# Moving clearing transfers and DRAM copies, and splitting the routing's and norm's small operations, in an mLSTM and mixture-of-experts kernel

## The chip, the cores and the metric

The kernel runs on one NeuronCore of a Trainium2 chip. The metric is device time in microseconds (us) for one execution; smaller is better. The core has a matrix engine (PE, TensorE), a vector engine (DVE), a scalar engine (ACT), a general engine (POOL, GpSimd) and a sequencer that mostly issues transfers (SP); each takes its own instructions in program order, and they wait for each other through semaphores. In the profile PE's clock stands at one of two levels, 2.4 GHz (granted clock 1.00) or 1.2 GHz (0.50).

## What is computed

Three layers follow each other. The reference, cut to its core (B=2, H=8, S=768, D=40, so 1536 tokens of 320 numbers; 8 experts):

```python
for t in range(S):                                    # an mLSTM, per batch and head
    m_new = maximum(f[t] + m, i[t]); f_s = exp(f[t] + m - m_new); i_s = exp(i[t] - m_new)
    C = f_s * C + i_s * outer(v[t], k[t]);  n = f_s * n + i_s * k[t]
    y[t] = sigmoid(o[t]) * (C @ q[t]) / maximum(abs(n @ q[t]), 1.0)
logits = x @ w_gate + log1p(exp(x @ w_noise)) * noise # router: two experts per token
out[token] = sum over its top 2 of weight * (relu(x @ w1[e]) @ w2[e])
final = (silu(x @ w_gate2) * (x @ w_val)) @ w_out     # a dense gated layer, 1536 wide
```

## The kernel before

**Attention.** The two sequences are cut into 12 chunks of 128 tokens (6 each, `j` from 0 to 11). A chunk is computed in the parallel form of the mLSTM, and a state is carried from chunk to chunk. The order of the work is written out by hand: strings of letters (`START`, `SECOND`, `BODY`, `LAST`, lines 61 to 65), in which a letter issues one piece for this chunk or for one that lies ahead. For chunk `j`, PE computes the scores `pS` (L275, one chunk ahead), the part from the carried state `py` (L297), the part within the chunk `pY` (L312) and the state's update (L322). ACT computes the weights `W` by an exponential from the broadcast gates `gbt` (`prep_w`, L265, two chunks ahead). DVE multiplies scores by weights (`weigh`, L281), adds the parts to `y` (`norm`, L338 to L344, where a maximum and a reciprocal make the divisor `dn`) and writes the chunk's output `x` in two multiplications (L355 and then L350). PE then transposes `x` (`gate_t`, L363) and multiplies it by the router's weights (`gate_l`, L372); the result is copied to `lg` (L373). In PE's order the transpose of chunk `j-1` stands ahead of `pY` of chunk `j`, so `pY` waits for `x` of the chunk before.

**Gates.** Running sums of the gates, `G_`, are written to DRAM as `gp` (four transfers, L206) and read back, broadcast to all partitions, as `gbt` (L176, from chunk 2 on).

**Routing.** After every three chunks `route` (L376) makes a list of 14 pieces: scale, noise, maxima, indices, one-hot, counts, PE's `place` (a prefix sum by small matmuls, L423 to L430), slots, weights. The letter `d` (`drip`, L486) issues the next piece. A piece holds up to six DVE instructions, and many read what the one ahead of them wrote. The last list is issued among the first steps of the experts, as the numbers in `SEQ` (L53) say. When a token's slot is known, POOL scatters its row to the expert's rows `xs` in DRAM (`scatter`, L474; letter `c`), two rows per token.

**Transfers.** SP issues nearly all transfers, in order, and waits ahead of many for a semaphore. Beside the loads of q and k (`QK`, L166), keys and values (`kvt`, L170), `gbt` and the expert weights (`stg`, L524), these are the clearing of `xs` with zeros (`clear`, L946: eight transfers of 384 rows and one of 320, letter `z`) and a copy of every chunk's output to DRAM (`keep`, L494, into `xd`). `xd` is read only where more tokens choose an expert than it has rows.

**Experts and dense layer.** 80 steps (10 groups of rows, 8 steps each, `step`, L901) and then 36 steps of the dense layer. The first step follows `xprep(0)` (L609), which transposes the rows `xgt` that were loaded back from `xs` (`xload`, L602) when the first 12 scatters had landed. POOL computes the low halves of some weight pieces (`wU`, `wV`, L542) already in the attention.

Of the kernel before, what the change touches and what calls it, by code (L numbers as in the profile page):

```python
# [23 lines left out]
E = 8  # L24
# [10 lines left out]
KD = 1  # L35
# [7 lines left out]
XL = 10  # L43
DU = (0, 1, 2)
# [16 lines left out]
START = 'gffhqkQlffffffff1cfrffff2dffsffffxoOffSffff34WKfTy5Gmfnafwfe6ffffŇŷ7ũŗŋűzųŮŭŶť'  # L61
LV = ()
SECOND = 'dGzcWSdiwydddqcdKactpcdsdnmvcldecd'
BODY = 'GKzcWSdiwddctpqdyacdsdnmdvclcdde'
LAST = 'iyddatdnpdmcdeslccdd'
# [23 lines left out]
def kernel(ctx, tc, qk, kvh, og, gates, cst, wgn, noise, w1, w2, w13, w2o, out):  # L89
# [286 lines left out]
    def route(t0, t1):  # L376
# [3 lines left out]
        def tile(shape, name, dt=F32):  # L380
            return rt.tile(shape, dt, name=f"{name}{n}", bufs=2)
# [14 lines left out]
        def noisy():
            v.tensor_tensor(out=Lg, in0=ex, in1=nz[:, t, :], op=OP.mult)
            v.tensor_tensor(out=Lg, in0=Lg, in1=lg[:, t, 0:E], op=OP.add)

        def top():  # L400
            for i in range(n):
                v.max(mx[:, i, :], Lg[:, i, :])

        def top_index():
            for i in range(n):
                v.max_index(ix[:, i, :], mx[:, i, :], Lg[:, i, :])

        def onehot():
            v.tensor_copy(xf, ix[:, :, 0:2])
            v.tensor_tensor(out=d, in0=mx[:, :, 1], in1=mx[:, :, 0], op=OP.subtract)  # L410
            v.tensor_tensor(out=oh[:, t].rearrange("p j k e -> p (j k) e"),
                            in0=iota_e[:, None, :].to_broadcast([128, 2 * n, E]),
                            in1=xf.rearrange("p j k -> p (j k)")[:, :, None].to_broadcast([128, 2 * n, E]),
                            op=OP.is_equal)

        def chosen():
            v.tensor_tensor(out=sel[:, t], in0=oh[:, t, 0], in1=oh[:, t, 1], op=OP.add)
            v.tensor_copy(selb[:, t], sel[:, t])
# [23 lines left out]
        def limits():  # L442
            v.tensor_tensor(out=pol[:, t], in0=ps_[0], in1=lim_c[:, b, None, :].to_broadcast([128, n, E]), op=OP.is_ge)
            v.tensor_tensor(out=pb, in0=ps_[0], in1=base_c[:, b, None, :].to_broadcast([128, n, E]), op=OP.add)

        def pick(k, src):
            def run():
                v.tensor_tensor(out=tm, in0=oh[:, t], in1=src().to_broadcast([128, n, 2, E]), op=OP.mult)
                v.tensor_reduce(so[:, k], tm, axis=AX.X, op=OP.add)
            return run  # L450
# [33 lines left out]
    spot = [0, 0]  # L484
# [416 lines left out]
    def step():  # L901
# [105 lines left out]
    def early_piece(j):  # L1007
# [10 lines left out]
        "n": (0, norm), "e": (0, emit_a), "m": (0, emit_b),  # L1018
# [12 lines left out]
    for j in range(NJ):  # L1031
# [8 lines left out]
        if j >= KD:  # L1040
            keep(j - KD)
# [128 lines left out]
```

## Time and profile before

| | |
|---|---|
| median of 3 runs | 558.68 us (554.36 to 561.88) |
| the profiled execution | 555.08 us, with a span of 553.4 us from its first to its last instruction |
| busy share of the span | PE 96%, DVE 68%, ACT 50%, POOL 26% |
| mean granted clock of PE | 0.959 |
| instructions | 9232 |
| bytes moved | 96.63 MB, mean 175 GB/s |

The profile is of one execution. A row of a timeline has the start in us from the beginning of the span, the busy time in us, engine, line, operation, what is written and from what, and a count of merged instructions; in brackets stands how long the engine had been idle and what ended that. The rows for a stretch give the busy time of each engine, PE's granted clock (1.00 is 2.4 GHz), the busy share of the DMA engines and the GB/s moved. A busy PE need not be a fast one: at a clock of 0.50 the same matmul is busy about twice as long.

### The profile page before, as it was taken

Reading aid. Unit: us, or ns where it says so; the run is one execution under the profiler, and the core shown is the slowest. Engines: PE = TensorE matmul, PEld = TensorE weight load, DVE = VectorE, ACT = ScalarE, POOL = GpSimd, SP = SyncE. Lnnn points to the kernel's source line nnn. Section 1 sums busy time; section 2 is a strip of 40 time slices with the busy share of each in tenths; the row PEclk is TensorE's granted clock in tenths of the full one; section 3 lists DMA queues with packets and bytes.
Section 4 is the critical chain, followed back from the end, with each engine's and each line's share of the span. In section 5 each row is a group of like instructions: output and inputs, shape, how many; then the busy total and the mean of one; then the engine's idle time right before and its main releaser. Section 6 shows DMA issues by size and latency. Waiting matters only on the chain. (4 is left out here: it accounts for less than half of the span.)

```text
span 553.4 us, 9232 instructions
## 1 busy us (share of the span) xinstructions
PE 529.3 (96%) x3333; PEld 478.8 (87%) x3335; DVE 373.8 (68%) x833; ACT 275.5 (50%) x593; POOL 145.2 (26%) x175
## 2 busy tenths in 40 slices
PE   8998779889999999999999999999999999999997
PEld 4687678879898999989999999888888888888886
DVE  5584977858688897989898867787643434443332
ACT  5464545235566776876877664554332223222221
POOL 4153675455004432232322235233000000000000
PEclk8798877969999999999999999999999999999999
DMA  8799965553758787988987686461001000010001
GB/s 247 214 332 356 304 236 161 168 196 113 295 171 320 259 281 255 330 296 277 317 292 254 214 280 227 160 233 49 0 1 49 0 1 0 2 47 1 1 0 47
DMA packets 36882, 96.63 MB, mean 175 GB/s; under 512 B 4848, under 2 KB 17936, under 8 KB 36832
## 3 DMA queue, kind: packets, MB, share of 16 engines
q1 hardware_dynamic: 32208, 83.55, 44.9%
q0 software_dynamic: 2304, 7.87, 4.3%
q10 hardware_dynamic: 2320, 4.58, 2.4%
q8 instruction: 27, 0.44, 0.3%
q14 instruction: 23, 0.19, 0.1%
HBM read 72.70 MB, written 23.28 MB: 173 GB/s over the span
## 5 line engine op out<-in xcount | busy, mean ns | idle before, releaser
L678 PE MATMUL py<-wV,h 128*128 128x320 f32 (+1 forms) x624 | 106.6, 312 | 1.2 <-ACT ysb L689 0.8
L678 PEld LDWEIGHTS py<-wV,h 128*128 128x128 f32 (+1 forms) x624 | 95.6, 185 | 2.7 <-ACT ysb L689 1.2
L641 PE MATMUL ph<-xh,wU 128*128 128x416 f32 (+1 forms) x320 | 91.5, 336 | 0.4 <-PEq L719 0.4
L581 POOL TENSOR_TENSOR cq<-cq,csg 128x512 f32<-128x512 f32 (+1 forms) x27 | 38.5, 1425 | 121.0 <-ACT cq L580 96.7
L839 DVE TENSOR_TENSOR sg<-pg,sg 128x512 f32<-128x512 f32 x36 | 24.9, 691 | 58.2 <-ACT sg L838 58.2
L860 PE MATMUL py<-wV,uh 128*128 128x320 f32 x288 | 63.8, 309 | 0.0
L641 PEld LDWEIGHTS ph<-xh,wU 128*128 128x128 f32 x320 | 59.6, 195 | 2.5 <-ACTq L719 0.7
L542 DVE TENSOR_TENSOR wU<-stg,wU 128x512 fp32r<-128x512 f32 x72 | 54.1, 776 | 6.7 <-ACT wU L541 6.2
L838 ACT ACTIVATE sg<-pg 128x512 f32<-128x512 f32 x36 | 21.5, 598 | 66.0 <-PE pg L641 61.2
L848 ACT ACTIVATE uh<-u 128x512 fp32r<-128x512 f32 x36 | 22.8, 633 | 62.0 <-DVE u L840 62.0
L641 PE MATMUL ph<-xl,wU 128*128 128x416 f32 (+1 forms) x160 | 52.3, 327 | 0.1
L860 PEld LDWEIGHTS py<-wV,uh 128*128 128x128 f32 x288 | 49.5, 188 | 3.0
L641 PE MATMUL pg<-x2h,wU 128*128 128x512 f32 x144 | 51.4, 397 | 0.0
L641 PE MATMUL pv<-x2h,wU 128*128 128x512 f32 x144 | 50.6, 392 | 0.0
L541 ACT ACTIVATE wU<-stg 128x512 fp32r<-128x512 f32 x78 | 46.4, 624 | 7.4 <-DVE yt L687 4.6
L650 ACT ACTIVATE h<-ph 128x416 fp32r<-128x416 f32 (+1 forms) x80 | 35.6, 445 | 19.5 <-PE ph L641 17.6
L860 PE MATMUL py<-wV,ul 128*128 128x320 f32 x144 | 44.4, 309 | 0.0
L542 DVE TENSOR_TENSOR wV<-stg,wV 128x640 fp32r<-128x640 f32 x42 | 37.6, 906 | 3.4 <-ACT wV L541 3.3
L641 PE MATMUL ph<-xr,wU 128*128 128x416 f32 (+1 forms) x160 | 39.3, 327 | 0.3 <-DVE wU L542 0.3
L849 DVE TENSOR_TENSOR ul<-u,uh 128x512 fp32r<-128x512 f32 x36 | 24.9, 690 | 19.9 <-ACT uh L848 19.9
L777 POOL DMA_INDIRECT gy<-yg,ig__89 x24 | 25.2, 1051 | 48.0 <-DVE wU L542 26.8
L840 DVE TENSOR_TENSOR u<-pv,sg 128x512 f32<-128x512 f32 x36 | 24.9, 691 | 17.1 <-PE pv L641 16.7
(175 smaller groups left out, 1065.6 us busy)
## 6 DMA issues: line engine op xcount, KB each, us to landing
stg<-in_w_dram SPq DMA_DIRECT2D x20, 768.0 KB
stg<-in_w_dram SPq DMA_DIRECT2D x20, 640.0 KB
cw<-in_w_dram SPq DMA_DIRECT2D x18, 512.0 KB
gbt<-gp SPq DMA_DIRECT2D x10, 512.0 KB
f<-cq SPq DMA_DIRECT2D x18, 256.0 KB
stg<-f SPq DMA_DIRECT2D x6, 768.0 KB
kvt<-in_kvh_dram SPq DMA_DIRECT2D x12, 324.0 KB
QK<-in_qk_dram SPq DMA_DIRECT2D x24, 160.0 KB
```

Of the source, the lines that this page charges most:

```text
L541: s.activation(hi[:, c], ST[u][:, c], AF.Copy)
L542: (g if lo_pool[0] else v).tensor_tensor(out=lo[:, c], in0=ST[u][:, c], in1=hi[:, c], op=OP.subtract)
L581: g.tensor_tensor(out=q, in0=q, in1=sg, op=OP.mult)
L641: pe.matmul(ps_ap, a, b, start=(i == 0), stop=(i == len(seq) - 1))
L650: s.activation(h[:, 0:C], p[:, 0:C], AF.Relu)
L678: pe.matmul(yp[0:nr, 0:DM], x_, w, start=st and i == 0, stop=sp and i == 2)
L777: g.indirect_dma_start(out=y, out_offset=None, in_=yg[0:NR0] if j < NC else yg, in_offset=bass.IndirectOffsetOnAxis(ap=ig_[:, j, k:k + 1], ...
L839: v.tensor_tensor(out=sg, in0=pg, in1=sg, op=OP.mult)
L840: v.tensor_tensor(out=u, in0=pv, in1=sg, op=OP.mult)
L848: s.activation(uh, u, AF.Copy)
L849: v.tensor_tensor(out=ul, in0=u, in1=uh, op=OP.subtract)
L860: pe.matmul(OP_[q][a][:, 0:DM], x_[:, t], w[:, c], start=(f == 0 and i == 0), stop=(f == 11 and i == 2))
```

## The change

It has three parts. **(1)** Four of the nine clearing transfers are issued right behind the first loads (`zz` in `START`); the two that stood at the end of `START` go, and later chunks issue 2, 2 and 1 in place of 2, 3 and 2. **(2)** The twelve copies to `xd` during the attention become two of 768 rows each, issued at steps 13 and 17 of the experts. **(3)** `route` returns about 36 single instructions, some of them empty places that only keep distance, in place of 14 pieces, and their order is new; the divisor's maximum and reciprocal (`norm_max`, `norm_rec`) are letters of their own; the strings have more `d`. `SEQ` is not changed.

```diff
-KD = 1
+KX = (13, 17)
-START = 'gffhqkQlffffffff1cfrffff2dffsffffxoOffSffff34WKfTy5Gmfnafwfe6ffffŇŷ7ũŗŋűzųŮŭŶť'
+START = 'gffhqkQlzzffffffff1cfrffff2dffsffffxoOffSffff34WKfTy5Gmfnafwfe6ffffŇŷ7ũŗŋűųŮŎōŭŶť'
-BODY = 'GKzcWSdiwddctpqdyacdsdnmdvclcdde'
+BODY = 'GKzcWSdiwdctpqdydacdsdndNmdMdvclcdedd'
...
-        v.reciprocal(dn, dn)
-        YN[j] = (y, dn)
+    def norm_rec(j):
+        dn = YN[j][1]
+        v.reciprocal(dn, dn)
...
-        return [scale, noisy, top, top_index, onehot, chosen, place, limits, pick(0, lambda: pol[:, t, None, :]),
-                pick(1, lambda: pb[:, :, None, :]), slots, carry, gap_exp, weights]
+        return [scale, None, tt(Lg, ex, nz[:, t, :], OP.mult), tt(Lg, Lg, lg[:, t, 0:E], OP.add), *tops,
...
+                lambda: s.activation(e2, d, AF.Exp),
+                tt(sel[:, t], oh_[:, :, 0], oh_[:, :, 1], OP.add),
+                lambda: v.tensor_copy(selb[:, t], sel[:, t]), total, place,
+                lambda: v.tensor_scalar(d, e2, 1.0, 1e-9, op0=OP.add, op1=OP.add),
+                *([tt(cs, cry, cs, OP.add)] if t0 else []),
+                lambda: v.reciprocal(wk_[:, :, 0], d), None,
...
+                tt(wk_[:, :, 1], e2, wk_[:, :, 0], OP.mult), slots, carry,
...
     def drip(k, last=False):
-        spot[0] += 1
         for _ in range(k):
-            if drq and (last or drq[0].__name__ != "place" or spot[0] > spot[1] + 1):
-                if drq[0].__name__ == "chosen":
-                    spot[1] = spot[0]
-                drq.pop(0)()
+            while last and drq and drq[0] is None:
+                drq.pop(0)
+            if drq:
+                f = drq.pop(0)
+                if f:
+                    f()
-    def keep(j):
-        sy.dma_start(xd[j * 128:(j + 1) * 128, :], x[:, j, 0:DM])
+    def keep(b):
+        sy.dma_start(xd[b * S:(b + 1) * S].rearrange("(j p) d -> p j d", p=128), x[:, b * NC:(b + 1) * NC, 0:DM])
...
+        if i in KX:
+            keep(KX.index(i))
...
-        if j >= KD:
-            keep(j - KD)
```

SP's order at the start of the program, before; the names are the transfers' targets and sources, `gp` and `gbt` the gates, `xs` the rows that are cleared:

```order
L170 DMA kvt<-in_kvh_dram 128x648
L206 DMA gp<-G__120 16x128 x3
L206 DMA gp<-G__120 16x3x128
L176 DMA gbt<-gp 128x1024
L166 DMA QK_113<-in_qk_dram 40x1024 x2
L170 DMA kvt<-in_kvh_dram 128x648
L985 DMA wg_t<-in_wgn_dram 128x3x16
L986 DMA nz<-in_noise_dram 128x96
L176 DMA gbt<-gp 128x1024
L166 DMA QK_111<-in_qk_dram 40x1024 x2
L949 DMA xs<-zt 384x1x320 x2
L170 DMA kvt<-in_kvh_dram 128x648
```

and the same place after the change:

```order
L171 DMA kvt<-in_kvh_dram 128x648
L942 DMA xs<-zt 384x1x320 x4
L207 DMA gp<-G__120 16x128 x3
L207 DMA gp<-G__120 16x3x128
L177 DMA gbt<-gp 128x1024
L167 DMA QK_113<-in_qk_dram 40x1024 x2
L171 DMA kvt<-in_kvh_dram 128x648
L978 DMA wg_t<-in_wgn_dram 128x3x16
L979 DMA nz<-in_noise_dram 128x96
L177 DMA gbt<-gp 128x1024
L167 DMA QK_111<-in_qk_dram 40x1024 x2
L171 DMA kvt<-in_kvh_dram 128x648
```

Four clearing transfers now stand ahead of the gates' way through DRAM, and none stands ahead of the fourth `kvt`.

DVE's order between the score product of chunk 6 (`W`, x2) and `y` of chunk 5, before (`so`, `nov`, `is_`, `cs`, `d`, `wk` are the routing's small tiles of the first three chunks):

```order
L281 TENSOR_TENSOR W_658<-pS,W_658 128x512 x2
L448 TENSOR_TENSOR tm_652<-oh,pb_650 128x48
L449 TENSOR_REDUCE so_651<-tm_652 128x6
L453 TENSOR_SCALAR nov_649<-so_651 128x6
L454 TENSOR_TENSOR so_651<-so_651,nov_649 128x6
L455 TENSOR_TENSOR so_651<-so_651,ck 128x6
L456 TENSOR_TENSOR is__88<-so_651 128x6
L434 TENSOR_REDUCE cs_653<-sel 128x8
L440 CAST cry<-cs_653 128x8
L304 TENSOR_TENSOR t_810<-py,eg 128x328
L463 CAST ig__89<-so_651 128x6
L464 TENSOR_SCALAR d_654<-e_655 128x3
```

(three more routing instructions follow ahead of `y`), and the same place after the change, from `W` on to `x`:

```order
L282 TENSOR_TENSOR W_656<-pS,W_656 128x512 x2
L420 TENSOR_TENSOR sel<-oh 128x24
L305 TENSOR_TENSOR t_789<-py,eg 128x328
L448 CAST selb<-sel 128x24
L426 TENSOR_REDUCE cs_650<-sel 128x8
L339 TENSOR_TENSOR y<-pY,t_789 128x328
L343 TENSOR_SCALAR dn<-y 128x8
L449 TENSOR_SCALAR d_651<-e_652 128x3
L348 TENSOR_TENSOR dn<-dn,y 128x8
L362 TENSOR_TENSOR x<-x,y 128x320
L451 RECIPROCAL wk<-d_651 128x3
L352 RECIPROCAL dn<-dn 128x8
```

Of the routing, 13 instructions stood between `W` and `y`; three do now, and the slots (`is_`) have moved to the chunk after this one.

DVE's order around the fourth step of the experts (the second `h` row below is that step's), before:

```order
L655 SCALAR_TENSOR_TENSOR h<-ph,h 128x224 x2
L397 TENSOR_TENSOR Lg_1439<-ex_1438,nz 128x24
L398 TENSOR_TENSOR Lg_1439<-Lg_1439,lg 128x24
L402 MAX mx_1440<-Lg_1439 128x8 x3
L406 MAX_INDEX ix_1441<-mx_1440,Lg_1439 128x8 x3
L409 CAST xf_1442<-ix_1441 128x6
L410 TENSOR_TENSOR d_1448<-mx_1440 128x3
L411 TENSOR_TENSOR oh<-ck,xf_1442 128x48
L417 TENSOR_TENSOR sel<-oh 128x24
L418 CAST selb<-sel 128x24
L655 SCALAR_TENSOR_TENSOR h<-ph,h 128x224
```

and after the change:

```order
L646 SCALAR_TENSOR_TENSOR h<-ph,h 128x224 x2
L420 TENSOR_TENSOR Lg_1424<-ex_1423,nz 128x24
L420 TENSOR_TENSOR Lg_1424<-Lg_1424,lg 128x24
L438 MAX mx_1425<-Lg_1424 128x8 x3
L439 MAX_INDEX ix_1426<-mx_1425,Lg_1424 128x8
L646 SCALAR_TENSOR_TENSOR h<-ph,h 128x224
L439 MAX_INDEX ix_1426<-mx_1425,Lg_1424 128x8 x2
L442 CAST xf_1427<-ix_1426 128x6
L420 TENSOR_TENSOR d_1433<-mx_1425 128x3
L420 TENSOR_TENSOR oh<-ck,xf_1427 128x48
L420 TENSOR_TENSOR sel<-oh 128x24
L448 CAST selb<-sel 128x24
```

The step's `h` now stands ahead of seven routing instructions that end in `selb`, the input of PE's `place`; PE's own order is the same here, `place` behind the fourth step.

## Rows read from the trace of the kernel before

**Rows 1.** Stretches: busy us per engine (count), PE's clock, DMA share, GB/s

```profile
core 0: us, PE busy (x) PEld busy (x) DVE busy (x) ACT busy (x) POOL busy (x), PEclk, DMA share, GB/s
12.00:16.00 4.00, 3.67 (x17) 3.50 (x19) 3.83 (x8) 4.00 (x3) 1.39 (x1) 0.50 0.50 153
...
28.00:58.00 30.00, 26.16 (x258) 23.97 (x254) 19.41 (x63) 16.85 (x53) 13.95 (x18) 0.89 0.98 335
...
58.00:116.00 58.00, 47.12 (x428) 43.09 (x425) 47.72 (x171) 26.14 (x78) 34.30 (x48) 0.85 0.60 199
...
131.00:553.00 422.00, 415.42 (x2423) 381.59 (x2421) 282.81 (x512) 214.05 (x418) 82.10 (x77) 1.00 0.46 156
```

**Rows 2.** Timeline of PE, the transpose of chunk 5's output

```profile
69.99 0.87 PE L363 MATMUL pg<-ck,x 128*128 128x128 f32 x3 [4.48 <-DVE x L350]
```

**Rows 3.** Stretches in which PE's clock stood at the lower level, columns as in rows 1

```profile
67.41:74.24 6.83, 4.25 (x23) 4.20 (x25) 3.46 (x12) 1.11 (x2) 6.21 (x11) 0.50 0.70 265
81.06:91.30 10.24, 10.24 (x68) 9.38 (x68) 8.65 (x42) 4.16 (x13) 3.96 (x5) 0.50 0.49 150
115.20:125.44 10.24, 9.78 (x40) 9.09 (x41) 4.10 (x22) 1.90 (x6) 5.94 (x12) 0.50 0.75 253
```

**Rows 4.** Timeline of SP's queue, two answers for short windows

```profile
17.06 0.38 SPq L176 DMA_DIRECT2D gbt<-gp  x1
...
28.15 0.36 SPq L170 DMA_DIRECT2D kvt<-in_kvh_dram  x1
```

**Rows 5.** Timeline of ACT, the weights of chunks 2 and 5

```profile
26.62 2.43 ACT L265 ACTIVATE W<-gbt,bc 128x128 f32<-128x128 f32 x8
...
44.68 2.45 ACT L265 ACTIVATE W<-gbt,bc 128x128 f32<-128x128 f32 x8 [4.30 <-DMA gbt<-gp]
```

**Rows 6.** DMA issues by line, count and size of one

```profile
xs<-zt SPq DMA_DIRECT2D x8, 480.0 KB
...
xd<-x SPq DMA_DIRECT2D x12, 160.0 KB
```

**Rows 7.** Timeline of DVE, small instructions that do and do not follow one another

```profile
56.25 0.30 DVE L402 MAX8 mx<-Lg 128x8 f32<-128x8 f32 x3
...
68.35 0.17 DVE L342 TENSOR_SCALAR dn<-y 128x8 f32<-128x8 f32 x1
68.56 0.17 DVE L343 TENSOR_TENSOR dn<-dn,y 128x8 f32<-128x8 f32 x1
```

**Rows 8.** Timeline of DVE from chunk 4's output to chunk 6's

```profile
60.82 0.48 DVE L350 TENSOR_TENSOR x<-x,dn 128x320 f32<-128x320 f32 x1
...
64.88 2.43 DVE L464 TENSOR_SCALAR d<-e 128x3 f32<-128x3 f32 x1
...
69.36 0.49 DVE L350 TENSOR_TENSOR x<-x,dn 128x320 f32<-128x320 f32 x1
...
75.61 1.42 DVE L342 TENSOR_SCALAR dn<-y 128x8 f32<-128x8 f32 x1
...
78.91 0.80 DVE L350 TENSOR_TENSOR x<-x,dn 128x320 f32<-128x320 f32 x1
```

**Rows 9.** Timeline of POOL beside the long instruction of rows 8

```profile
65.72 1.54 POOL L542 TENSOR_TENSOR wV<-stg,wV 128x640 fp32r<-128x640 f32 x1
```

**Rows 10.** Timelines of DVE, POOL, SP and PE: from chunk 9 to the experts

```profile
99.64 0.49 DVE L338 TENSOR_TENSOR y<-pY,t 128x328 f32<-128x328 f32 x1
...
100.11 0.99 POOL L476 DMA_INDIRECT xs<-x,is__88  x1 [0.17 <-issue]
...
102.64 1.74 SPq L607 DMA_DIRECT2D xgt<-xs  x4
...
113.21 0.81 PE L624 MATMUL pxt<-ck,xgt 128*128 128x128 f32 x6
115.57 0.87 PE L363 MATMUL pg<-ck,x 128*128 128x128 f32 x3 [1.56 <-DVE x L350]
```

**Rows 11.** Timelines of DVE and PE at the fourth step of the experts

```profile
126.83 0.39 DVE L655 SCALAR_TENSOR_TENSOR h<-ph,h 128x224 fp32r<-128x224 f32 x1 [0.18 <-ACT h L650]
...
127.11 0.19 PE L423 MATMUL pr<-selb,slt 128*128 128x24 bf16 x1
```

More of the change, by code (lines that the diff above doesn't have):

```diff
@@ L390, in route @@
         ps_ = []
+        oh_, wk_ = oh[:, t], wk[:, t]
+        ohr = oh_.rearrange("p j k e -> p (j k) e")
         def scale():
@@ L394, in scale @@
             s.activation(ex, ex, AF.Ln, bias=1.0)
[L396 to L418, printed above, removed]
         def place():
@@ L431, in place, with tt, limit, total @@
                           start=False, stop=True, skip_group_check=True)
+        def tt(out, in0, in1, op):
+            return lambda: v.tensor_tensor(out=out, in0=in0, in1=in1, op=op)
+        def limit(out, lim, op):
+            return lambda: v.tensor_tensor(out=out, in0=ps_[0], in1=lim[:, b, None, :].to_broadcast([128, n, E]), op=op)
+        def total():
+            v.tensor_reduce(cs, sel[:, t].rearrange("p j e -> p e j"), axis=AX.X, op=OP.add)
         def carry():
-            v.tensor_reduce(cs, sel[:, t].rearrange("p j e -> p e j"), axis=AX.X, op=OP.add)
-            if t0:
-                v.tensor_tensor(out=cs, in0=cry, in1=cs, op=OP.add)
             if t1 == NC:
@@ L440, in carry @@
                 v.tensor_copy(cry, cs)
[L442 to L450, printed above, removed]
@@ L469, in route @@
-        return [scale, noisy, top, top_index, onehot, chosen, place, limits, pick(0, lambda: pol[:, t, None, :]),
-                pick(1, lambda: pb[:, :, None, :]), slots, carry, gap_exp, weights]
+        tops = [lambda i=i: v.max(mx[:, i, :], Lg[:, i, :]) for i in range(n)]
+        tops += [lambda i=i: v.max_index(ix[:, i, :], mx[:, i, :], Lg[:, i, :]) for i in range(n)]
+        tm2 = tile([128, n, 2, E], "tn")
+        return [scale, None, tt(Lg, ex, nz[:, t, :], OP.mult), tt(Lg, Lg, lg[:, t, 0:E], OP.add), *tops,
+                lambda: v.tensor_copy(xf, ix[:, :, 0:2]),
+                tt(d, mx[:, :, 1], mx[:, :, 0], OP.subtract),
+                tt(ohr, iota_e[:, None, :].to_broadcast([128, 2 * n, E]),
+                   xf.rearrange("p j k -> p (j k)")[:, :, None].to_broadcast([128, 2 * n, E]), OP.is_equal),
+                lambda: s.activation(e2, d, AF.Exp),
[4 more added lines that the diff above has]
+                lambda: v.reciprocal(wk_[:, :, 0], d), None,
+                limit(pol[:, t], lim_c, OP.is_ge), limit(pb, base_c, OP.add),
+                tt(tm, oh_, pol[:, t, None, :].to_broadcast([128, n, 2, E]), OP.mult),
+                tt(tm2, oh_, pb[:, :, None, :].to_broadcast([128, n, 2, E]), OP.mult),
+                lambda: v.tensor_reduce(ov, tm, axis=AX.X, op=OP.add),
+                lambda: v.tensor_reduce(sl, tm2, axis=AX.X, op=OP.add),
+                lambda: v.tensor_scalar(nov, ov, -1.0, 1.0, op0=OP.mult, op1=OP.add),
+                tt(ov, ov, dump_c[:, :, t].rearrange("p k j -> p j k"), OP.mult),
+                tt(sl, sl, nov, OP.mult),
+                tt(wk_[:, :, 1], e2, wk_[:, :, 0], OP.mult), slots, carry,
+                lambda: v.tensor_copy(ig_[:, t], sl),
+                tt(wn[:, t], wk_, nov, OP.mult)]
@@ L1051 @@
             xprep(0)
-    for j in range(NJ - KD, NJ):
-        keep(j)
     gate_t(NJ - 1)
```

25 lines of the change are left out of this document (8 added, 17 removed).

## The prediction

> **What bounds the kernel now.** I read the stretches first, then who waits for whom on PE, and last the timelines of the engines waited for. In the stretches [rows 1] the reader is to see two programs. From 131 us on PE is busy 415.42 of 422.00 us at full clock: 6.6 us of idle, so nothing there can give much, and what changes the time is when this stretch begins. Before it, from 28 to 58 us the DMA engines are busy for 0.98 of the time and move 335 GB/s; from 58 to 116 us their share is 0.60, DVE is busy 47.72 of 58 us and PE 47.12 at a mean clock of 0.85. So the attention has a part held by transfers and then a part held by DVE.
>
> In the second part PE's longest idle is 4.48 us, ahead of the transpose of chunk 5's output, ended by DVE's last multiplication for it [rows 2]. After such idles the clock stands at the lower level, 1.2 GHz: 6.83, 10.24 and 10.24 us long [rows 3]. At half speed the 10.24 us that PE is busy in the second of them hold 5.1 us of work.
>
> **Part 1, the clearing transfers.** Four of 480 KB [rows 6] are 1.97 MB, at 335 GB/s 5.9 us of the DMA engines. They go to where the share is lowest, 0.50 from 12 to 16 us [rows 1], which looks free. But the gates' transfers `gp` stand behind them in SP's queue now, and `gbt` of chunk 2 waits for them; SP issued it at 17.06 us [rows 4]. How late it becomes no row shows. Above, the full 5.9 us; below, 3.9, if the idle half of those 4 us is used in full. I take 5, the middle, and `gbt` is issued at about 22 us. ACT needed it at 26.62 [rows 5], so nearly all of this is covered, and SP stood at 28.15 waiting for a buffer of `kvt` anyway [rows 4], so it has caught up by then. What shows I put at +1.0 us, between 0 (all covered) and +4.5 (hardly any cover, as the load's own time is not known).
>
> What is won later by four transfers fewer? ACT waited 4.30 us for `gbt` at 44.68 [rows 5], with the DMA engines full. The bytes to be moved by 58 us are the same but for the copies to `xd`; the gap at the start that was filled opens again behind 17 us, where `gbt`, `QK` and `kvt` of chunk 2 start 5 us later. So the queue at 28 us is as long as before, and I put 0 here; below -5.9.
>
> **Part 2, the copies.** Five of 160 KB [rows 6] by 58 us are 0.8 MB, 2.4 us of DMA time at 335 GB/s, worth something only where PE waits for `gbt` and not for its own slow clock: I put 0 and leave 2.4 as a bound. SP's waits for a chunk's output go, but the next load of `kvt` waits for PE's state update of nearly the same time. In the experts the two transfers of 0.98 MB take 2.9 us each, in a stretch with a DMA share of 0.46 [rows 1]: hidden. If one stood right ahead of a weight transfer that is needed at once, up to 2.9 us; I take 0.
>
> **Part 3, the small operations.** Of two DVE instructions of 0.17 us in which the second reads the first, the second starts 0.21 us after it (68.35 to 68.56); three that don't read each other take 0.30 us together [rows 7], 0.10 each. Alternation is thus worth 0.11 us for each pair that is broken up. The Trainium skill says otherwise at first reading: "VectorE: DVE Perf Modes", section "The DRAIN you can't avoid", has the next instruction wait until the pipeline is empty and holds that this can't be skipped by leaving out semaphores. By that rule breaking up pairs is worth nothing and the gain below is 1.7 us smaller. The same section lets an instruction that nothing holds start earlier, and the three maxima in 0.30 us agree with that exception and not with the rule.
>
> *Chunk 5.* From the end of chunk 4's output (60.82 + 0.48 = 61.30) to that of chunk 5 (69.36 + 0.49 = 69.85) DVE took 8.55 us [rows 8]. In it one instruction on 128x3 numbers was busy 2.43 us, 2.26 more than its like, and ended with a weight piece of POOL (65.72 + 1.54 = 67.26) [rows 8, 9]. Of the routing, 15 instructions stood in this stretch and 9 do now: 6 x 0.17 = 1.0 us. Six pairs broken up: 0.7. Without the long one that is 8.55 - 2.26 - 1.0 - 0.7 = 4.6. POOL's pieces stay, so I add back half of a stall, 1.1: 5.7, a gain of 2.8 us (1.7 to 3.9). With it most of the 4.48 us of PE's idle goes. Late next is PE itself.
>
> *Chunk 6.* Its output ended at 79.71 [rows 8], 9.86 us later. In the stretch 67.41 to 74.24 PE was busy 4.25 us at half clock [rows 3]; if the idle ahead of it shrinks to some 1.5 us, the clock stays, which gives half, 2.1 us (0 to 2.1). The divisor that was busy 1.42 us [rows 8] I leave.
>
> *Chunks 7 and 8.* The second slow stretch costs 5.1 us. It too followed idles behind DVE. I take half, 2.6 us, since each later idle can bring the clock down again (0 to 5.1).
>
> *Chunks 9 to 11.* Three broken pairs each, 9 x 0.11 = 1.0 us, and half of a stall of 1.3 us: 1.6 (0 to 2.3).
>
> *Into the experts.* The slots of the second three chunks are ready a good chunk later: 1.5 us behind `y` of chunk 9 in place of ahead of it. Then six scatters of 0.99 us with gaps of about 0.25 [rows 10], a weight piece of 1.54 between them: 9.0 us; 1.5 us to SP's load (101.10 to 102.64), and some 2.5 for it to land (0.9, half of SP's four issues, to 10.6, when the transposes came): 99.64 + 1.5 + 9.0 + 1.5 + 2.5 = 114.1 us on the old clock. The transposes `pxt` were at 113.21, ahead of the last chunk's (115.57) [rows 10]; PE has them behind it now. What filled a wait of 1.56 us now lies on the path: 0.81 us and about 1.0 for the copies behind it, +1.8 us (0 to 4).
>
> *The last routing.* `SEQ` still says 6 and 2, which were pieces and are now single instructions. So the fourth step's `h` on DVE stands ahead of two indices and five more instructions up to `selb`: 126.83 + 0.39 + 7 x 0.17 = 128.4 us. PE's `place` ran at 127.11 [rows 11] and has the next step's matmuls queued behind it, so PE stands 1.3 us (0.9 to 1.8), at full cost.
>
> **Sum.** +1.0 - 2.8 - 2.1 - 2.6 - 1.6 + 1.8 + 1.3 = -5.0 us. Against the profiled execution's 555.08 that is 550.1 us; the median of the runs shown is 3.6 us higher, 558.68, and on it I forecast 553.7 us. The runs shown lie 7.5 us apart, and the state of the clock differs between executions, I suppose; 2% (11.2 us) is about what a measurement can tell here.
>
> **Rivals.**
> Slower: *the gates come too late.* If `gbt` of chunk 2 lands clearly after 26.62 us, ACT, and behind it PE, waits between 26 and 40 us, and the clock falls there instead of later, when the kernel has no slack: +4.5 for the wait, +5.1 for a slow stretch as long as the longest, +1.3 and +1.8 at the end, -2.8 - 1.6 kept: +8.3, 567.0 us. For it speaks that all of SP's first loads are issued in one row and `gbt` waits for a write to DRAM that is last in it; against it the 9.6 us between 17.06 and 26.62. It decides from a landing about 1 us after 26.62.
>
> No change: *the stalls move with POOL.* DVE's long instructions end with POOL's work, and POOL does as much as before, so each piece meets another of the many small instructions. Then of part 3 only the instructions moved and the pairs remain: -1.7 - 1.0 and +1.0 + 1.8 + 1.3 make +1.4, 560.1 us. The Trainium skill states such a rule: "SBUF — State Buffer", section "SBUF: two separate sides", calls the port pair of VectorE and GpSimd an exclusive lock that the first to start holds for a whole instruction. Rows 8 and 9 agree with it, and by it nothing in this change lessens the stalls but chance.
>
> Faster: *the clock holds.* With the idle of chunk 5 gone no slow stretch comes before 115 us: -3.9 - 2.1 - 5.1 - 2.3, and +1.3 at the end, 12.1 us, 546.6. For it speaks that from 91 to 115 us the clock held through idles of about 1 us; against it that the attention of before has slow stretches in its first part too (mean clock 0.89 from 28 to 58 us [rows 1]), which the change hardly touches.
>
> Smaller: *broken pairs are worth nothing.* Without 0.7 for chunk 5 and 1.0 for chunks 9 to 11 the sum is -3.3, 555.4 us; the starts at 0.10 and 0.21 us [rows 7] speak against it. This is the rule of the first page of the Trainium skill named above.
>
> **Chances.** The forecast 0.45, the stalls that move 0.22, the clock that holds 0.18, the late gates 0.12, the pairs 0.03. The forecast's own range, half a term up or down, is 549 to 557; with the fast and the level case, and a part of the slow one, 545 to 563 us. Faster by over 2% (under 547.5) has most of the fast case and a little of the forecast's edge, 0.14; slower by over 2% (over 569.9) the tail of the gates' case, 0.03; the rest 0.83.
>
> **What would show it.** Right: `gbt` issued at 21 to 23 us and no wait of ACT at 26 us; PE's idle ahead of chunk 5's transpose under 2 us; `place` of the last routing waiting some 1.3 us for `selb`; `pxt` behind the last transpose of `x`; the experts starting some 6 us earlier. Wrong: PE idles between 28 and 40 us, a slow stretch before 50 us, or long DVE instructions beside POOL's pieces that add up to as much as before (then the gain is chance); a weight transfer in the experts for which PE stands; or waits for `gbt` that have shrunk by several us, so that the first part was worth more than nothing.

## The result and the profile after

| | before | after |
|---|---|---|
| median of 20 runs each, one chip | 557.99 us (553.64 to 565.68) | 552.91 us (547.39 to 559.67) |
| ratio | | 0.9912, 95% interval 0.9889 to 0.9935 |
| the profiled execution | 555.08 us, span 553.4 us | 547.39 us, span 545.7 us |
| mean granted clock of PE in it | 0.959 | 0.984 |

The kernel became 5.1 us faster by the medians, 0.9%; 5.0 were forecast. The ratios leave out the slow runs, those more than 1.5% above the fastest of their kernel. The profiled execution after the change is the fastest of its 20, so its 7.7 us are not the usual gain. Its stretches, columns as in [rows 1]:

```profile
12.00:16.00 4.00, 3.84 (x25) 2.48 (x25) 3.79 (x9) 4.00 (x3) 0.75 (x1) 0.93 1.04 348
28.00:58.00 30.00, 27.82 (x276) 25.74 (x274) 19.20 (x62) 18.30 (x59) 14.40 (x19) 0.89 0.92 322
58.00:116.00 58.00, 46.26 (x438) 42.04 (x437) 46.22 (x176) 25.71 (x78) 38.59 (x56) 0.94 0.61 202
131.00:546.00 415.00, 409.54 (x2375) 375.37 (x2374) 277.71 (x504) 210.44 (x410) 76.22 (x67) 1.00 0.47 160
```

The gap at the start is filled (DMA share 0.50 before, full now), from 28 to 58 us the DMA engines have some air (0.98 to 0.92), and PE's mean clock from 58 to 116 us rose from 0.85 to 0.94. Where [rows 3] have stretches of 6.83 and 10.24 us at half clock, this execution has short ones:

```profile
29.62:33.03 3.41, 3.41 (x19) 3.41 (x17) 0.94 (x3) 2.45 (x8) 2.06 (x4) 0.50 1.03 337
50.10:53.51 3.41, 3.41 (x17) 3.41 (x18) 1.12 (x2) 2.46 (x9) 0.64 (x1) 0.50 0.74 286
101.30:104.71 3.41, 3.21 (x18) 2.94 (x18) 1.61 (x10) 0.40 (x2) 0.90 (x2) 0.50 0.23 76
111.54:114.95 3.41, 3.41 (x17) 3.41 (x17) 0.46 (x2) 0.36 (x1) 2.91 (x5) 0.50 0.66 250
```

To see where the time came from I cut both executions at the same events: DVE's copy `lg` of the router's result of chunk 0, of chunk 3, of chunk 10, and PE's last `place`. First the kernel before, then the changed one, columns as in [rows 1]:

```profile
35.20:60.60 25.40, 21.97 (x203) 19.97 (x201) 15.34 (x54) 13.24 (x42) 9.32 (x11) 0.87 0.97 334
60.60:115.30 54.70, 44.21 (x397) 40.54 (x397) 44.74 (x158) 24.50 (x74) 33.02 (x46) 0.84 0.60 201
115.30:127.10 11.80, 11.44 (x53) 10.64 (x53) 5.38 (x31) 2.34 (x8) 5.84 (x12) 0.57 0.66 222
127.10:553.40 426.30, 419.32 (x2457) 385.47 (x2455) 286.17 (x533) 216.22 (x424) 83.49 (x79) 1.00 0.45 155
```

```profile
36.00:57.70 21.70, 19.88 (x205) 18.37 (x203) 14.87 (x47) 13.50 (x43) 9.46 (x11) 0.92 0.87 307
57.70:106.30 48.60, 38.38 (x395) 34.99 (x394) 41.31 (x154) 23.08 (x68) 31.89 (x45) 0.96 0.59 193
106.30:119.60 13.30, 9.83 (x59) 8.81 (x59) 7.21 (x44) 3.49 (x13) 7.35 (x13) 0.87 0.57 199
119.60:545.70 426.10, 419.65 (x2455) 385.28 (x2454) 284.82 (x532) 216.16 (x424) 82.65 (x79) 1.00 0.47 159
```

Read the second column, the length: start +0.8, chunks 0 to 3 -3.7, chunks 3 to 10 -6.1, the entry to the experts +1.5, the rest -0.2; together -7.7 us, the whole difference of the spans. DVE worked 3.4 us less in the seven chunks and stood 2.7 us less.

The signs the prediction named, first on SP and ACT (to compare with [rows 4, 5]):

```profile
7.39 5.46 SPq L942 DMA_DIRECT2D xs<-zt  x4
13.07 4.70 SPq L207 DMA_DIRECT2D gp<-G__120  x4
21.34 0.34 SPq L177 DMA_DIRECT2D gbt<-gp  x1
...
26.50 0.35 SPq L171 DMA_DIRECT2D kvt<-in_kvh_dram  x1
```

```profile
25.87 2.45 ACT L266 ACTIVATE W<-gbt,bc 128x128 f32<-128x128 f32 x8 [0.92 <-DMA gbt<-gp]
...
44.96 2.45 ACT L266 ACTIVATE W<-gbt,bc 128x128 f32<-128x128 f32 x8 [3.69 <-DMA gbt<-gp]
51.05 2.45 ACT L266 ACTIVATE W<-gbt,bc 128x128 f32<-128x128 f32 x8 [2.15 <-DMA gbt<-gp]
```

`gbt` of chunk 2 is issued at 21.34 us (forecast 21 to 23), and ACT starts with it at 25.87, not late against the 26.62 of before (it was itself ready 0.92 us earlier). The wait for chunk 5 went from 4.30 to 3.69 us, that for chunk 6 to 2.15; the forecast saw no gain there. Before, chunk 6 had waited 4.20 us:

```profile
52.81 2.45 ACT L265 ACTIVATE W<-gbt,bc 128x128 f32<-128x128 f32 x8 [4.20 <-DMA gbt<-gp]
```

Then PE, at chunk 5 and at the entry (to compare with [rows 2, 10, 11]):

```profile
65.00 0.52 PE L370 MATMUL pg<-ck,x 128*128 128x128 f32 x3 [0.59 <-DVE pb L423]
...
107.45 0.44 PE L615 MATMUL pxt<-ck,xgt 128*128 128x128 f32 x2 [0.40 <-ACT xgt L606]
109.33 0.37 PE L632 MATMUL ph<-xl,wU 128*128 128x224 f32 x1 [1.12 <-DVE xl L618]
...
119.64 0.17 PE L409 MATMUL pr<-selb,slt 128*128 128x24 bf16 x1 [2.00 <-DVE selb L448]
```

The idle of 4.48 us ahead of chunk 5's transpose is 0.59, `pxt` stands behind the last transpose, 5.8 us earlier than the 113.21 of before, and the last `place` waits 2.00 us for `selb` (1.3 were forecast). All this was forecast in kind. What was not is on DVE and POOL:

```profile
60.75 1.53 DVE L448 CAST selb<-sel 128x24 bf16<-128x24 f32 x1
...
76.79 0.15 DVE L439 FIND_INDEX8 ix<-mx,Lg 128x8 uint32<-128x8 f32 x1
76.87 2.06 DVE L357 TENSOR_TENSOR x<-x,dn 128x320 f32<-128x320 f32 x1
78.84 0.15 DVE L442 CAST xf<-ix 128x6 f32<-128x6 uint32 x1
...
81.24 3.23 DVE L329 TENSOR_TENSOR Cs<-Cs,dec 128x164 f32<-128x164 f32 x1
```

```profile
60.72 1.53 POOL L533 TENSOR_TENSOR wV<-stg,wV 128x640 fp32r<-128x640 f32 x1 [1.07 <-ACT wV L532]
...
77.29 1.27 POOL L533 TENSOR_TENSOR wU<-stg,wU 128x512 fp32r<-128x512 f32 x1
...
81.12 0.73 POOL L288 TENSOR_TENSOR KS<-kvt,eg 128x320 f32<-128x320 f32 x1
81.80 1.21 POOL L268 TENSOR_SCALAR_AFFINE_SELECT W<-W 128x512 f32<-128x512 f32 x2
82.99 1.25 POOL L533 TENSOR_TENSOR wU<-stg,wU 128x512 fp32r<-128x512 f32 x1
```

`selb` was busy from 60.75 to 62.28 us, as long as POOL's weight piece beside it (60.72 to 62.25); its like takes 0.17. The multiplication that makes `x` of chunk 7 was busy 2.06 us where its like takes 0.47, and ended 0.37 us behind another weight piece (77.29 to 78.56); the 3.23 us of `Cs` (its like 0.31) cover four of POOL's instructions, 81.12 to 84.24. The stretched instruction of chunk 5 [rows 8] is gone, and others stand in its place.

So three of the signs that the prediction named for being wrong came too: a slow stretch before 50 us (29.62), waits for `gbt` that shrank by 2.7 us in sum, and long DVE instructions beside POOL's work that add up to as much as before (11.0 us, before 9.7, in the table below). The last was to mean that the gain is chance. The runs say otherwise: the chunks 3 to 10 took 47.1 to 49.6 us in all six executions with the new order and POOL's work unchanged, and 53.6 to 55.2 in the five with the old one.

### The profile page after: what moved, and what is told of

It is laid out like the page before. It is cut to its first block, busy times and chain, and to the rows that moved or that the text cites. A ratio compares the mean times of both kernels' runs of the same rounds, so it can differ in the third digit from the quotient of the medians.

```text
span 545.7 us, 9215 instructions
## 1 busy us (share of the span) xinstructions
PE 519.2 (95%) x3333; PEld 469.0 (86%) x3335; DVE 369.7 (68%) x833; ACT 275.5 (50%) x593; POOL 144.5 (26%) x175
## 5 line engine op out<-in xcount | busy, mean ns | idle before, releaser
L829 ACT ACTIVATE sg<-pg 128x512 f32<-128x512 f32 x36 | 21.5, 598 | 65.9 <-PE pg L632 60.4
L839 ACT ACTIVATE uh<-u 128x512 fp32r<-128x512 f32 x36 | 22.8, 633 | 62.1 <-DVE u L831 62.1
L632 PE MATMUL ph<-xr,wU 128*128 128x416 f32 (+1 forms) x160 | 39.3, 326 | 1.7 <-issue 1.2
L768 POOL DMA_INDIRECT gy<-yg,ig__89 x24 | 25.5, 1062 | 46.5 <-DVE wU L533 26.2
```

The costliest lines, as they stand in the source:

```text
L632: pe.matmul(ps_ap, a, b, start=(i == 0), stop=(i == len(seq) - 1))
L768: g.indirect_dma_start(out=y, out_offset=None, in_=yg[0:NR0] if j < NC else yg, in_offset=bass.IndirectOffsetOnAxis(ap=ig_[:, j, k:k + 1], ...
L839: s.activation(uh, u, AF.Copy)
```

## The experiments

Each was timed beside the kernel before on its own chip (medians there 554.8, 555.8 and 555.8 us in the three groups of four). The columns are lengths in us from the trace of one execution, cut at the events above: from the start to the router copy of chunk 0, from there to that of chunk 3, to that of chunk 10, to the last `place`. "Stretch" adds up, over chunks 3 to 10, what each DVE instruction was busy beyond the shortest of its line, tiles and form there. All lengths are of one execution of each kernel; the ratios of e1 to e12 are of 12 executions each (e10: 6).

| run | ratio to before | start | 0 to 3 | 3 to 10 | stretch | to `place` |
|---|---|---|---|---|---|---|
| before | | 35.2 | 25.4 | 54.7 | 9.7 | 11.8 |
| after | 0.991 (0.989 to 0.994) | 36.0 | 21.7 | 48.6 | 11.0 | 13.3 |
| e1 part 3 | 0.997 (0.994 to 1.001) | 38.0 | 24.7 | 49.6 | 13.1 | 14.5 |
| e2 part 1 | 0.999 (0.996 to 1.002) | 39.3 | 24.7 | 53.7 | 9.8 | 11.0 |
| e3 part 2 | 1.002 (0.998 to 1.006) | 35.1 | 25.6 | 54.8 | 11.1 | 11.0 |
| e4 before, idle matmuls | 0.996 (0.993 to 1.000) | 38.0 | 26.2 | 55.2 | 9.0 | 8.3 |
| e5 after again | 0.991 (0.987 to 0.994) | 41.2 | 22.3 | 47.4 | 11.4 | 13.5 |
| e6 parts 1, 2 | 1.000 (0.996 to 1.004) | 36.6 | 24.3 | 53.6 | 8.5 | 11.3 |
| e7 two waits removed | 0.991 (0.987 to 0.995) | 37.1 | 23.0 | 47.6 | 11.9 | 12.7 |
| e8 chain order | 1.006 (1.002 to 1.010) | 37.0 | 22.2 | 50.0 | 11.2 | 19.3 |
| e9 pairs | 0.995 (0.992 to 0.998) | 37.0 | 22.0 | 50.3 | 9.2 | 14.6 |
| e10 no halves on POOL | 0.983 (0.977 to 0.989) | 42.4 | 22.8 | 43.2 | 6.3 | 12.6 |
| e11 e7 and idle matmuls | 0.994 (0.990 to 0.997) | 36.9 | 22.7 | 47.1 | 11.0 | 13.0 |
| e12 parts 1, 3 | 0.993 (0.990 to 0.996) | 35.1 | 23.5 | 48.2 | 9.5 | 14.3 |

**The parts alone.** e1 is the changed kernel with the clears and copies of the kernel before, e2 and e3 are the kernel before with one part each (the lines are those of the diff above).

> Part 3 alone: the routing and the norm as single instructions in the new order; the clearing transfers and the copies to xd stay as before. Theory A (as forecast: parts 1 and 2 are worth about nothing): this kernel has the whole gain, 552 to 553 us beside a kernel before at 558, a ratio of 0.989 to 0.992; PE's idle of 4.48 us ahead of chunk 5's transpose is under 1 us, and the stretches at half clock between 58 and 116 us add up to under 10 us (before: 6.83, 10.24 and most of a third). Theory B (the clearing transfers at the start and their absence later carry it): at most half of the gain, a ratio above 0.995. Theory C (chance: any shift of DVE's small instructions against POOL's pieces decides which chunk is held): the stalls land elsewhere again, the time is anywhere between 552 and 560 us and the idles stand ahead of other chunks than in the changed kernel.

> Part 1 alone: four clearing transfers behind the first loads, the rest later; routing, norm and copies as before. Theory A (the forecast's +1.0 and 0): 558 to 560 us, a ratio of 1.000 to 1.003, gbt of chunk 2 issued at 21 to 22 us, and the idle of 4.48 us ahead of chunk 5's transpose still over 3.5 us. Theory B (the clears carry the gain): a ratio under 0.996, fewer half-clock stretches, chunk 5's transpose with less than 2.5 us of idle. Theory C (chance): idles ahead of other chunks than before and a ratio off 1.000 by more than 0.004 in either direction.

> Part 2 alone: the twelve copies to xd during the attention become two during the experts; clears, routing and norm as before. Theory A (hidden on both sides): 557 to 559 us, a ratio of 0.998 to 1.002, and no idle of PE over 0.5 us at steps 13 to 20 of the experts. Theory B (SP's waits for a chunk's output held the loads, or the copies' bytes held gbt): a ratio of 0.994 to 0.997, ACT's waits for gbt of chunks 3 to 6 shorter by 2 us or more in sum. Theory C (the two copies of 0.98 MB hold a weight transfer): a ratio of 1.003 to 1.006 with PE idle in the experts.

Part 3 has the gain of chunks 3 to 10 (-5.1 us) in every version that holds it and in none that doesn't; parts 1 and 2 leave them at 53.6 to 54.8. That much of theory A of the first run holds. The whole gain is not there: 0.997, theory B's ratio, with an interval that holds 1, and e1 had about 20 us at half clock between 58 and 116 us where under 10 were expected. Parts 1 and 2 are no measurable gain alone. Part 1 does what the prediction put at 0, all the same: ACT's wait for `gbt` of chunk 6 is 3.8 to 4.2 us in the four executions without the early clears and 0.5 to 3.0 in the ten with them. The idle ahead of chunk 5's transpose was no fixed thing either: 1.94 us in e2 and 1.27 in e3, with 2.38 us ahead of the first `place` in its stead. Part 2 moved something that was to be hidden: one look at the experts of e3 (ACT, DVE, then PE) shows

```profile
157.56 0.68 ACT L570 ACTIVATE cq<-cw 128x512 f32<-128x512 f32 x1 [2.67 <-DMA cw<-in_w_dram]
```

```profile
158.27 0.43 DVE L571 TENSOR_SCALAR cq<-cq 128x512 f32<-128x512 f32 x1 [1.69 <-ACT cq L570]
```

```profile
160.90 0.52 PE L672 MATMUL py<-wV,h 128*64 128x320 f32 x2 [1.18 <-DVE ysb L691]
```

a wait of 1.18 us nine us behind the second copy's issue (151.57), and from the last `place` to the end the nine executions with the copies in the experts take 426.1 to 428.9 us (mean 427.4), the five without 423.5 to 427.0 (mean 425.4). So 2 us, on the mean of single executions. The copies hold the load of `cw`: ACT waited 1.5 to 2.8 us for it in eight of the nine (0.57 in e8) and at most 0.4 in the five. But PE stood behind it, waiting for `ysb` as here, in five of the nine only, 1.0 to 1.2 us, and not in the first execution of the changed kernel; that the whole 2 us are the copies' is not shown.

**The clock by itself.** e4 adds `warm(p, WARM.get(j, 0), 384, 128)` ahead of the transposes in `gate_t`, with `WARM = {5: 64, 6: 32, 9: 16, 11: 24}`.

> The kernel before, with idle matmuls (64, 32, 16 and 24 of 128 columns in bf16, whose result nobody reads; 3.4, 1.7, 0.85 and 1.3 us of PE at full clock) in PE's queue right ahead of the transposes of chunks 5, 6, 9 and 11, where PE stands idle for 4.48, 2.07, 1.11 and 1.56 us. Nothing that DVE or POOL do is changed. Theory A (half of what the change brought is clock: PE falls to 1.2 GHz after those idles and stays there while it has work): the stretches at half clock at 67, 81 and 115 us shrink or go, the last transposes come 3 to 6 us earlier, the time falls by 3 to 5 us, a ratio of 0.991 to 0.995. Theory B (DVE's chain alone sets the time, the clock follows it): the outputs x of chunks 5 to 11 end when they ended before within 1 us, ratio 0.999 to 1.003. Theory C (the idle matmuls stand in the way where the wait has moved): slower by up to 3 us, a ratio up to 1.006.

```profile
64.20:119.40 55.20, 48.34 (x533) 45.26 (x533) 43.70 (x158) 24.42 (x74) 32.78 (x46) 0.94 0.59 192
119.40:127.70 8.30, 7.36 (x54) 6.63 (x54) 5.13 (x31) 2.46 (x8) 5.79 (x12) 1.00 0.88 296
```

PE's mean clock over the seven chunks rose from 0.84 to 0.94 and they took 55.2 us, as before: there DVE's chain sets the time and the clock follows (theory B). At the entry, where PE is busy nearly all the time, full clock makes 8.3 us of 11.8. So both theories hold, each for its stretch, and I put the ratio of 0.996 down to the entry.

**The changed kernel again, and parts 1 and 2 together.** e5 has no edit; e6 is e2 with e3.

> The changed kernel once more, on the chip and in the hour of the three runs beside it, as their yardstick. Theory A (the gain is real and the same on each chip): a ratio of 0.989 to 0.994. The trace shows whether the short stretches at half clock of its first profile (five of 3.41 us, 17 us in all) are its usual state or a lucky execution: if usual, 17 to 25 us again and 75 to 77 us from the router copy of chunk 0 to that of chunk 11; if lucky, 30 us or more at half clock, while the chunks still take 75 to 78 us because DVE's chain and not the clock sets them.

> Parts 1 and 2 together, routing and norm as before. From the router copy of chunk 2 to that of chunk 3 the kernel before took 11.8 us, part 3 alone 11.0, part 1 alone 10.7, part 2 alone 10.6, all three 8.6. Theory A (this stretch is held by transfers, and only fewer bytes from both parts bring gbt of chunk 6 early): it takes 8.4 to 9.6 us here, ACT's wait for gbt of chunk 6 is 2 to 3 us, the next two stretches stay at 8.7 and about 9 as in the kernel before, and the time is 2 to 3 us under before, a ratio of 0.994 to 0.997. Theory B (the gain needs part 3's faster DVE): 10.3 us or more, a ratio of 0.998 to 1.002.

From chunk 0 to the last `place` e5's lengths are those of the first execution within 1.3 us, yet its span is 553.3 us, 7.6 longer: 2.8 us of that lie behind `place`, and the start is 5.2 us longer. Its stretches at half clock behind the start add up to 17.1 us (13.7 in the first execution, 34.1 before), so the short ones are this kernel's usual state. What happened at the start: the clock's records of this execution begin at 30.67 us, and its matmuls until there run at half speed. The same 16 matmuls, of the first execution and of e5:

```profile
12.50 2.05 PE L235 MATMUL pG<-G__120,ck 16*128 16x128 f32 x16
```

```profile
14.21 3.78 PE L235 MATMUL pG<-G__120,ck 16*128 16x128 f32 x16
```

This phase ends between 12.6 and 34 us in the fourteen executions, and the start takes 35.1 to 42.4 us; e5, e2 and e10, where it ends last (30.7 to 34.2), have the longest starts (39.3 to 42.4). e6 falls for theory B: chunk 2 to chunk 3 takes 10.8 us, not 8.4 to 9.6.

**The waits that were left, and the order on DVE.** e7 sets `SEQ = (0, 0, 17, 0, -99)` and issues `xprep(0)` ahead of `drip(99, True)`. e8 and e9 put `route`'s instructions back in the order of dependence and cluster the letters:

```diff
-BODY = 'GKzcWSdiwdctpqdydacdsdndNmdMdvclcdedd'
+BODY = 'GKzcWSiwddctpqydddacsdddnNMmvclcddedd'
-LAST = 'idydatdndNmdMpcdeslccddd'
+LAST = 'iyddatdddnNMmpcdeslccddd'
```

> The changed kernel with the numbers of SEQ counted in single instructions (17 of the last list ahead of the fourth step, so that selb is made ahead of that step's h and place follows behind the step), and with the preparation of the first expert's rows ahead of the rest of the third routing. Theory A (the waits that the change left lie on PE's path): PE's wait for selb (2.00 us) goes under 0.3 and that for xl (1.12 us) under 0.4, the time falls by 1.5 to 3 us against the changed kernel run beside it, a ratio to before lower by 0.003 to 0.005. Theory B (PE has slack there, or the routing's later work makes a new wait of the same size): the same ratio as the changed kernel within 0.001, with a new idle of over 1 us in the first eight steps of the experts.

> The changed kernel with the same single instructions of routing and norm, but in the order of dependence and in clusters, so that the next reads what the one ahead of it wrote: of neighbours on DVE between the router copies of chunks 0 and 11, 78 are such pairs (91 in the kernel before, 36 in the changed one). Theory A (a dependent start costs 0.11 us more than a free one): 42 pairs by 0.11 are 4.6 us of DVE; from the router copy of chunk 0 to that of chunk 11 it takes 3 to 5 us longer than the changed kernel beside it, a ratio to before of 0.994 to 1.000. Theory B (the dependence costs nothing, what counts is when the work is issued and how it is spread): within 1 us of the changed kernel's chunks, and the same ratio within 0.002.

In e7 both waits went, and the ratio stayed, as theory B has it, but without the new idle that B named; the intervals are too wide to exclude the 0.003 of theory A. PE's row from the copy of chunk 10 to `place`:

```profile
107.70:120.40 12.70, 12.08 (x60) 10.81 (x60) 6.26 (x43) 3.23 (x12) 6.37 (x12) 0.63 0.58 204
```

PE is busy 12.08 us in place of 9.83, at a clock of 0.63 in place of 0.87: what the waits gave went to the clock in this execution. e8 was confounded: its slots came one letter too late, so one scatter fell behind the chunk's others (110.61 us), and with it

```profile
115.46 1.47 PE L617 MATMUL pxt<-ck,xgt 128*128 128x128 f32 x6 [5.74 <-DMA xgt<-xs]
```

which is the wait that the prediction priced at 1.8. e9 is e8 with one multiplication moved behind the slots (which restores the order on all engines but DVE).

> The changed kernel with DVE's routing and norm instructions in the order of dependence and in clusters, corrected so that PE, ACT, POOL and SP have exactly the changed kernel's order; only DVE's differs. Between the router copies of chunks 3 and 10 there are 69 neighbours on DVE of which the second reads what the first wrote in the kernel before, 22 in the changed one, 54 here. Theory A (a dependent start costs 0.11 us): 32 pairs by 0.11 are 3.5 us; these seven chunks, 54.7 us in the kernel before and 47.4 to 48.6 in the changed one, take 50.5 to 52.5, and the ratio to before is 0.995 to 0.999. Theory B (the pairs are worth nothing; what the spreading brought is when work is issued): 47 to 49 us, a ratio of 0.990 to 0.993.

The rows of e9's DVE show what a dependent start looks like (the reciprocal 0.21 us behind the maximum that it reads, the multiplication that it doesn't feed 0.12 behind it), and that multiplication takes this chunk's stall:

```profile
79.33 0.17 DVE L348 TENSOR_TENSOR dn<-dn,y 128x8 f32<-128x8 f32 x1
79.54 0.20 DVE L352 RECIPROCAL dn<-dn 128x8 f32<-128x8 f32 x1
79.66 2.11 DVE L362 TENSOR_TENSOR x<-x,y 128x320 f32<-128x320 f32 x1
```

The seven chunks take 50.3 us, 2.2 more than the mean of the six runs with the new order (after, e1, e5, e7, e11, e12: 48.1), a little below theory A's range; the ratio is in it. The stretch differs too. Taken off, e9 has 41.1 us and e8, whose DVE has nearly the same order, 38.8; the six have 35.7 to 38.7, mean 36.8, and the five with the old order 43.7 to 46.2, mean 44.8. So 32 pairs cost 2.0 to 4.3 us, 0.06 to 0.13 each, and the 47 pairs that the change broke are worth 3 to 6 of its 8.0 us. Some 0.7 us of the rest, at 0.17 each, are four instructions fewer between the two copies (158 and 154 in the rows above). What remains I can't say: in the old order up to eight small instructions stood in a row ahead of what PE waits for, and no run tries that alone.

**POOL's halves.** In e10 ACT writes `lo` with `scale=0.0` where POOL subtracted, so it leaves out the low halves.

> The changed kernel without POOL's low halves of the weight pieces during the attention: ACT writes zeros there (the output lacks those low halves, the transfers stay). POOL loses 8 subtractions of 1.3 to 1.54 us between 56 and 116 us, ACT gets as many copies of 0.6 to 0.7. Theory A (DVE's stretched instructions beside POOL's subtractions hold the chunks): of the about 10 us by which DVE's instructions are longer than their like between chunks 3 and 11 more than 4 go, the chunks 3 to 10 take 44 to 46.5 us in place of 47.4 to 48.6, the ratio to before is 0.984 to 0.988. Theory B (the stretching moves to POOL's other work, the scatters and the masks, or PE waits for something else): less than 2 us of the stretching goes, 47 to 49 us, 0.989 to 0.993.

```profile
65.20:108.40 43.20, 37.73 (x390) 34.66 (x388) 37.16 (x154) 27.24 (x76) 23.09 (x38) 0.96 0.64 214
```

Seven subtractions, 10.0 us of POOL, are missing in the seven chunks; the stretch falls from 11.0 to 6.3, the length by 5.4 from 48.6 (4.9 against the mean), although ACT is busy 4.2 us more. Theory A, and beyond its range. The rest of the stretch stands beside POOL's masks, `KS` and scatters.

**What is left.** e11 is e7 with `warm` ahead of the part from the carried state, `{8: 16, 10: 32}`; e12 is the changed kernel with the copies of before.

> The changed kernel with SEQ in single instructions and the first expert's rows prepared ahead of the rest of the third routing (as in the run with these two alone, which had the changed kernel's ratio and lost its 3.1 us of waits to a stretch of 10.24 us at half clock), and besides with 16 and 32 idle matmuls of 128 columns (0.85 and 1.7 us at full clock) in PE's queue ahead of the part from the carried state of chunks 8 and 10, where PE stands for 1.7 and 1.8 to 2.7 us. Theory A (the clock at the entry of the experts took the gain): no stretch at half clock from 95 to 125 us, waits for selb and xl under 0.4 us, a ratio to before of 0.984 to 0.988. Theory B (PE's waits there are covered, or the idle matmuls are in the way): 0.989 to 0.993.

> Parts 1 and 3 together, the copies to xd as before: what is left of the question why part 3 alone gave 0.997, parts 1 and 2 together 1.000 and all three 0.991. Theory A (the clears are what part 3 needs: the stretch from the router copy of chunk 2 to that of chunk 3 is freed by four clears fewer, the copies are worth nothing): this stretch takes 7 to 9.5 us, a ratio of 0.990 to 0.993. Theory B (the copies count as much as the clears): 10 to 11 us, a ratio of 0.994 to 0.998. Theory C (the differences of a few us between these versions are the executions' clock at the start and not the parts): the stretch is as in one of the two, but the ratio does not follow it.

e11 has no gain over the changed kernel (0.994): a stretch of 6.83 us at half clock at 110 us came all the same, so theory B, a little above its range. It was the only one between 21.5 and 140 us, and that brought nothing: another sign that the clock does not hold the chunks. e12 agrees with theory A: 0.993, and 7.5 us from chunk 2 to 3, though chunk 1 to 2 took 9.2 there; over the three chunks it has 23.5 us, between part 3 alone (24.7) and all three (21.7 to 23.0). The ratios of e1 and e12 alone would not part them, their intervals overlap. Among the versions with the full computation none beats the changed kernel.

## Why the prediction was right, and where only its sum was

The time came out, and so did the class (no change beyond 2%). Several terms did not, and that they cancelled is luck.

- **Gates late, +1.0: not contradicted, but not shown.** The ten executions with four early clears reach chunk 0's copy at a mean of 37.9 us, the four others at 36.6; +0.8 in the profiled pair. But the clock's first phase ends 1.5 us later in the ten on the mean, and where it ends at the same time, 18.9 us, e12 with the clears takes 35.1 us to that copy and e3 without them 35.1 too: the delay was covered there. The late-gates rival needed `gbt` of chunk 2 about 1 us after 26.62; ACT had it at 25.87.
- **Later transfers and copies, 0: wrong.** Chunks 0 to 3 won 3.7 us in the profiled pair, and 22.4 on the mean of the seven executions with all of the parts 1 and 2 and single instructions, against 25.4. The step that failed is "the queue at 28 us is as long as before, and I put 0 here". The bound there was -5.9. The four clears fewer shorten the wait for `gbt` of chunk 6, as the runs of part 1 show; the chunks gain by it only with part 3 (e6: 24.3). Given back: some 2 us in the experts, up to 1.2 of them by the copies as far as the rows show, which I had put at 0 with 2.9 as a bound.
- **Chunk 5, -2.8: right in size, wrong in working.** It took 6.03 us by its outputs (57.92 + 0.90 to 64.85) in place of 8.55. But "POOL's pieces stay, so I add back half of a stall" fails as a rule for the whole: the stretch over chunks 3 to 10 is 11.0 us after 9.7. The rival of the stalls that move had this mechanism right, and e10 shows that they stand on the path at about full price. The Trainium skill's rule in "SBUF — State Buffer", section "SBUF: two separate sides", is an exclusive lock on the port pair of VectorE and GpSimd that the first to start holds for a whole instruction. `selb`, which began 0.03 us behind POOL's piece and ended 0.03 us behind its end, agrees with it. But DVE's instruction did not come second everywhere: `x` of chunk 7 began 0.42 us ahead of the piece that it outlasted, and `d` of [rows 8, 9], which the prediction read as agreeing, 0.84 us ahead. A scatter was under way on POOL both times; whether it held DVE no run shows.
- **Why that rival's time (560.1) was nevertheless wrong, and the main step that failed:** "Six pairs broken up: 0.7" and "three broken pairs each, 9 x 0.11". I counted 15 pairs where I had looked; by the order of DVE's instructions 69 dependent neighbours stood between the copies of chunks 3 and 10 and 22 do now. The price, 0.11 us, lies in what e8 and e9 show (0.06 to 0.13); the count was a third. The rule of "VectorE: DVE Perf Modes", section "The DRAIN you can't avoid", in the Trainium skill, has the next instruction wait for an empty pipeline, with the exception that one which is not held starts earlier. e9's multiplication, which starts 0.08 us before the reciprocal ahead of it ends, agrees with the exception and not with the rule.
- **Chunks 6 to 8, -2.1 and -2.6 for the clock: wrong.** e4 has the clock without the gain. Of what chunk 6 won (9.86 to 5.51 us), 2.6 us are three stretched instructions that stood in it before (1.42 us at 75.61 and 0.80 at 78.91 [rows 8], and 1.22 at 77.06 between them); the remaining 1.7 I put down to DVE's shorter chain. Chunks 7 and 8 won 0.2 us, for there the stalls of 2.06 and 3.23 us stand now. The clock counts at the start and at the entry, where PE has work without a gap.
- **Chunks 9 to 11, -1.6: wrong.** From the end of chunk 8's output to that of chunk 11's it took 19.0 us before and after.
- **Into the experts, +1.8: too much, and `place`, +1.3: 2.0 and 2.1 in the changed kernel's two executions, 1.1 to 1.2 in e1, e9 and e12.** `pxt` waits 0.40 us and in e5 not at all, since the last transpose is early as well; e8 shows that the margin is one scatter. A wait of 1.12 us for `xl` behind the rest of the third routing was not foreseen. Together the entry is 1.5 us longer, although its clock is 0.87 and was 0.57.

So the sum of -5.0 was met by -5.1 out of larger terms of both signs: on the means of the executions +1.3 at the start, in part the clock's, -3.0 in the chunks 0 to 3, -6.3 in 3 to 10, about +2 at the entry and +2.0 behind it. These add up to -4.0 us; the other 1.1 us is what single executions leave open.

## What to carry to other kernels

On an engine that sets the time with small instructions, count the dependent neighbours over the whole stretch from the order of the instructions, not in the one place that the profile drew the eye to; each broken pair gave 0.06 to 0.13 us here. A stall beside another engine is not removed by moving its victim: add up the stretching before and after, and look for the work that causes it (10 us of POOL's subtractions cost 5 us here). A slow clock cost its price here only where the engine had work without a gap; fill one idle and measure before counting it.

## What I had not expected

- The clock's first phase at half speed ended at 12.6 us in one execution of the changed kernel and at 30.67 in another, though PE was busy for 10.00 of the 10 us from 10 to 20 us in the second, and 5 us of the span hung on it; the start differs between executions by as much as the change is worth.
- In e5, e8, e9 and e10 the rows of a stretch say clock 1.00 where the matmuls show half speed, because the clock's records begin later (20.6 to 34.2 us); the duration of a repeated matmul is the safer reading there.
- Waits on PE's path that went (3.1 us in e7) did not measurably shorten the run: the clock of the same stretch fell from 0.87 to 0.63.
